# A block-attention and MLP kernel: the newest of a slot's three neighbouring value blocks is loaded by GpSimd, the sampled blocks stay with SyncE

## The chip, the core and the metric

The kernel runs on one core of a Trainium2 chip. The metric is the device time of one execution in microseconds (us), the median of several runs. Engines are named as the profile names them: PE is TensorE, DVE is VectorE, ACT is ScalarE, POOL is GpSimd, SP is SyncE. SP does no arithmetic; it issues transfers. POOL computes and can issue transfers as well.

## The reference, cut to what matters

```python
# attention: 4 batches, 8 heads, 768 rows in 24 blocks of 32, head size 64
scores = scale * q @ k.T
mask = (|blk_i - blk_j| <= 1) | first or last block, of rows or of columns
mask |= blk_j in sampled_blocks[blk_i]        # 3 sampled blocks per block row
attn = softmax(where(mask, scores, -1e9))
out = attn @ v
# then, with x = out as 3072 tokens x 512
h = x @ w_in                                  # 512 x 2048
g = s * maximum(h, 0) ** 2 + b
result = g @ w_out                            # 2048 x 512
```

`sampled_blocks` is an input, so which blocks are sampled is known only when the kernel runs.

## The kernel before, in words

**Slots.** Attention runs in 52 slots, in the order that the table entry "ORD" (L31) gives. Eight dense slots do the two block rows that see every key (the first and the last). The other 44 are sparse: a sparse slot does one of the 22 inner block rows for one of two batch pairs, `e` = 0 or 1 (all eight heads of two batches at once). The block rows of a pair are three streams that walk along neighbouring block rows, A and C upwards, B downwards; while all three are alive their slots alternate C, A, B, and when C has ended only A and B alternate.

**Values of a slot.** A sparse row needs its three neighbouring blocks, the first and last blocks, and three sampled ones. The three neighbours of a stream lie in one row of the tile `vA` (`window_values`), at place j % 3. From one slot of a stream to its next two neighbours stay, and only the newest block comes in, over the one that has gone out: `window_v` (L778), one transfer, 32 partitions x 2 batches x 512 numbers. It may start only when the previous slot of the same stream has finished its product with the values. Only the first slot of a stream in a pair, called `entire` in the code, loads all its window, in several transfers; 21 of the 59 transfers at L778 are of that kind. The sampled blocks go to a ring of five rows, mostly in `vB`, by `sampled_v` (L874, three transfers whose source comes from a register; L871 renews the last block once per ring row in the second pair). Keys are handled alike, but on chip: whole key tiles `kt` are loaded by SP (L697), and POOL copies the newest block (`window_k`, L891) and the sampled ones (`sampled_k`, L902) into the tile `kk`. Queries of the sparse slots are loaded by POOL (L714).

**A sparse slot** then runs so: scores on PE (L958), subtracting the maximum on DVE (L976, results `ptile` and `nm`), exponential on ACT (L989), transposes on PE (L1018; L1016 for dense ones), evacuation by DVE (L1034) or ACT (L1036), the product with `vA` and `vB` on PE into `xs` (`av`, L1075, 64 multiplications), scaling on DVE (L1081), transposes on PE (L1087), a copy on ACT (L1092), and a spill to memory by SP (L1099). Dense slots use L937, L1026 and L1065 in the corresponding places. PE's order per slot i is: transposes of i, last transposes of i - 1, scores of i + 2, product with the values of i.

**Weights.** Beside attention, `decode_f64` (L40) splits blocks of `w_in` and `w_out` into high and low parts: SP loads a raw block in two halves (L59, `raw_i` and `raw_o`), DVE (L85, L87), POOL (L88) and ACT work on it. After attention comes the MLP: products L440 to L442, L482 to L484 and L619 on PE, which read the attention's result back (L400).

**What sets the order.** Each engine runs its instructions in the order in which the program issues them. That order comes from `Plan` (L109), which simulates the engines before anything is issued: each operation has an engine, a cost in ns, a priority (for loads, the slot that needs them less a lead, "VL" 11 for windows and "GV" 13 for sampled blocks) and dependencies. On each engine the earliest possible operation with the smallest priority goes next. The costs steer the order only; on the chip everything waits for its real dependencies, in that order. In the letters of the plan, "s" is SP and "g" is POOL.

Of the kernel before, what the change touches and what calls it, by code (L numbers as in the profile page):

```python
# [108 lines left out]
class Plan:  # L109
# [15 lines left out]
    def op(self, eng, cost, prio, fn, deps=(), alloc=(), use=(), order=(), nbytes=0, cols=0, late=0.0):  # L125


        o = Plan.Op()
        o.cost, o.prio, o.fn, o.nbytes, o.cols, o.late = cost if isinstance(cost, dict) else {eng: cost}, prio, fn, nbytes, cols, late
        o.pick = isinstance(cost, dict)  # L130
        o.deps, o.order, o.alloc = [d for d in deps if d], [d for d in order if d], alloc
        o.end, o.seq = None, len(self.ops)
        for k in (*alloc, *use):
            self.users.setdefault(k, []).append(o)
        self.ops.append(o)
        return o
# [76 lines left out]
def kernel(  # L213
# [16 lines left out]
    nc = tc.nc  # L230
# [432 lines left out]
    with ExitStack() as es:  # L663
# [12 lines left out]
        for w in T["ORD"].split():  # L676
            if w[1] == "D":
                slots.append(("d", "abcd".index(w[0]), int(w[2]), 0))
            else:
                r = "ABC".index(w[1])  # L680
# [37 lines left out]
        def value_tiles():  # L718
            if "A" not in vbox:
                for z in "AB":  # L720
                    vbox[z] = gp.tile([P, 4, 2, DM], F32, tag="vg", name=f"v{z}", bufs=2)

        def window_values(r):
            value_tiles()
            return vbox["A"][:, r]

        def sampled_values(n):
            value_tiles()
            return vbox["B"][:, n - 1] if n else vbox["A"][:, NST]
# [11 lines left out]
        def block_rows(e, j, n=1):  # L741

            return v[2 * e:2 * e + 2, j * BLK:(j + n) * BLK, :].rearrange("a r d -> r a d")

        def newest(k):
            return k - 1 if STREAMS[1] >= k > STREAMS[1] - 8 else k + 1
# [23 lines left out]
        def newcomers(k, entire):  # L770
            return list(range(k - 1, k + 2)) if entire else [newest(k)]

        def window_v(i, entire, m):

            _, e, k, r = slots[i]
            js = newcomers(k, entire)
            j, p = (js[m], js[m] % 3) if m < len(js) else (0, NSL)
            nc.sync.dma_start(out=window_values(r)[p::4], in_=block_rows(e, j))  # L778


        ident = pers.tile([P, P], F32, name="ident")
# [63 lines left out]
        def load_registers(eng):  # L845
            _, regs[eng] = nc.values_load_multi_w_load_instructions(
                packed[0:1, 1:NB - 1], engines=[eng], min_val=0, max_val=NB32 ** NSL - 1, bass_reorder=False,
                skip_runtime_bounds_check_because="three numbers of 0..NB-1, clamped on the chip")

        def block_register(eng, k, a):  # L850

            n = regs[eng][k - 1] >> (5 * a) if a else regs[eng][k - 1]
            return (n & (NB32 - 1) if a < NSL - 1 else n).with_bounds(min_val=0, max_val=NB - 1)
# [4 lines left out]
        def ring_row(what, i):  # L858
            if i not in ring[what]:
                ring[what][i] = len(ring[what]) % {"k": KG, "v": VG}[what]  # L860
            return ring[what][i]

        def sampled_v(i, a):


            _, e, k, r = slots[i]
            row = ring_row("v", i)
            vt = sampled_values(row)
            if a == 0 and holds["v"].get(row) != e:
                holds["v"][row] = e  # L870
                nc.sync.dma_start(out=vt[NSL::4], in_=block_rows(e, NB - 1))  # L871
            src = v[2 * e:2 * e + 2].rearrange("a (n e) d -> n e a d", e=BLK)
            j = block_register(mybir.EngineType.SP, k, a)
            nc.sync.dma_start(out=vt[a::4], in_=src[bass.ds(j, 1)].rearrange("o e a d -> (o e) a d"))  # L874
# [9 lines left out]
        def window_k(i, entire):  # L884

            _, e, k, r = slots[i]
            kk = keys_tile()
            if entire:
                nc.gpsimd.tensor_copy(flat(kk[:, r, NSL:NSL + 1]), flat(kts[e][:, :1]))
            for j, p, n in runs(k, entire):  # L890
                nc.gpsimd.tensor_copy(flat(kk[:, r, p:p + n]), flat(kts[e][:, j:j + n]))  # L891

        def sampled_k(i, a):

            _, e, k, r = slots[i]
            row = ring_row("k", i)
            kg = keys_tile()[:, NST + row]
            if a == 0 and holds["k"].get(row) != e:
                holds["k"][row] = e
                nc.gpsimd.tensor_copy(flat(kg[:, NSL:]), flat(kts[e][:, NB - 1:]))  # L900
            j = block_register(mybir.EngineType.Pool, k, a)
            nc.gpsimd.tensor_copy(flat(kg[:, a:a + 1]), flat(kts[e][:, bass.ds(j, 1)]))  # L902
# [207 lines left out]
        op = plan.op  # L1110
# [27 lines left out]
        o_rs = op("s", 4400, T["RS"], lambda: load_registers(mybir.EngineType.SP), [o_si])  # L1138
# [18 lines left out]
        def parts_of(e, blocks):  # L1157
            return [kld[(e, y, p)] for p in sorted({j * KPS[e] // NB for j in blocks}) for y in range(2)]
# [9 lines left out]
        for i, (kind, e, k, r) in enumerate(slots):  # L1168
            u, cost, col = unit_of[i], costs[kind], cols[kind]
# [21 lines left out]
            if dense:  # L1191
                s_use.append((f"kt{e // 2}", e // 2))
            else:
                prev = before.get(r)
                entire = k == STREAMS[r]
                first = not before
                blocks = [*range(k - 1, k + 2), 0] if entire else [newest(k)]
                new = [("kk", "kk")] if first else []
                pk = op("g", 1900 if entire else 430, u - T["GK"], lambda i=i, w=entire: window_k(i, w),
                        [*parts_of(e, blocks), *(prev[0] if prev else [])], alloc=new, use=[(f"kt{e}", e)] + ([] if first else [("kk", "kk")]), order=[pk])  # L1200
                s_deps.append(pk)
                first_pk = first_pk or pk
                queries()
                for a in range(NSL):
                    pk = op("g", 460, u - T["GK"] + 0.1 * (a + 1), lambda i=i, a=a: sampled_k(i, a), [o_rg, *parts_of(e, range(NB))],
                            alloc=[] if a else [("kg", i)], use=[(f"kt{e}", e), ("kk", "kk")] + ([("kg", i)] if a else []), order=[pk])
                    s_deps.append(pk)
                s_use += [("kk", "kk"), ("kg", i)]

                vt = [("vg", "vA"), ("vg", "vB")]  # L1210
                if first:
                    for m in range(5):
                        pvl = op("s", 450, -8.3 + 0.02 * m, lambda m=m: global_values(m), alloc=[] if m else vt, use=vt if m else [],
                                 order=[pvl], nbytes=(131e3 if m == 4 else 200e3))
                        globs.append(pvl)
                av_deps += globs if e == 0 else []
                for m in range(len(newcomers(k, entire)) + (entire and e > 0)):
                    pvl = op("s", 450, -8.2 + 0.02 * m if first else u - T["VL"] + 0.1 * m, lambda i=i, w=entire, m=m: window_v(i, w, m), prev[1] if prev else [],
                             use=vt, order=[pvl], nbytes=131e3)
                    av_deps.append(pvl)  # L1220
                for a in range(NSL):
                    pvs = op("s", 520, u - T["GV"] + 0.1 * a, lambda i=i, a=a: sampled_v(i, a), [o_rs],
                             alloc=[] if a else [("vs", i)], use=[*vt, *([("vs", i)] if a else [])], order=[pvs], nbytes=131e3)
                    av_deps.append(pvs)
                pv_at.append((u, pvs))
                if 0 <= i - T["K1"] < KPS[1]:
                    key_piece(1, None, i - T["K1"], u - T["GV"] + 0.4, [pvs])
                av_use = [*vt, ("vs", i)]
# [77 lines left out]
            if k % NBC == 1:  # L1306
                left = sum(sl[0] == "s" and sl[1] == e and sl[2] % NBC == 1 for sl in slots[i + 1:])
                done[e] = done.get(e, 0) + 1
                for b in (2 * e, 2 * e + 1):
                    g = (k - 1) // NBC // 6  # L1310
# [95 lines left out]
        for k in range(NPL):  # L1406
            g, f = subs[k]
# [6 lines left out]
            if k > 0:  # L1414
                g, f = subs[k - 1]
# [45 lines left out]
    for i in range(NPL, NSUB):  # L1461
        g, f = subs[i]
# [10 lines left out]
    for s in range(S0, B):  # L1473
        a, b = 2 * s, 2 * s + 1
        for p in range(NFC // 2):
            for n in (1, 2, 6, 7, 5, 3, 4):
                to = product(p, s, n)
                i = None
# [4 lines left out]
                elif n == 2:  # L1483
                    i = take((a, p), to, part_sums["m1"], ALU.add)
# [4 lines left out]
                elif n == 5:  # L1489
                    i = take((b, p + 8), to, part_sums["u2"], ALU.add)  # L1490
                    vec.tensor_tensor(out=part_sums["u3"], in0=to, in1=part_sums["u1"], op=ALU.add)
                elif n == 3:
                    i = take((b, p), to, part_sums["u3"], ALU.add)
                else:
                    i = take((a, p + 8), part_sums["u2"], to, ALU.subtract)
# [93 lines left out]
```

## Time and profile before

| what | value |
|---|---|
| median of three runs | 802.42 us (802.12 to 802.53) |
| profiled execution | 802.29 us |
| its span | 800.5 us |
| mean granted clock of PE | 0.979 |
| busy: PE, DVE, ACT, POOL | 740.6, 573.1, 480.3, 242.1 us |
| transfers on the hardware queue (issued by SP) | 81.76 MB, 34.8% of 16 engines' span |
| transfers on the software queue (issued by POOL) | 6.29 MB, 2.8% |

The span is what the profiler recorded, from the first to the last instruction; the profiled execution's own time is 1.8 us more. Attention takes the first 276 us or so, the MLP the rest. In rows of the timeline the columns are start, length (us), engine, line, operation, output <- inputs, count, and in brackets how long the engine was idle before and what ended that. SPq is the part of SP that issues transfers. In rows of waits there are the engine and its line, what it waited for, and then total us, times, longest us.

### The profile page before, as it was taken

Reading aid. Unit: us, or ns where it says so; the run is one execution under the profiler, and the core shown is the slowest. Engines: PE = TensorE matmul, PEld = TensorE weight load, DVE = VectorE, ACT = ScalarE, POOL = GpSimd, SP = SyncE. Lnnn points to the kernel's source line nnn. Section 1 sums busy time; section 2 is a strip of 40 time slices with the busy share of each in tenths; the row PEclk is TensorE's granted clock in tenths of the full one; section 3 lists DMA queues with packets and bytes.
Section 4 is the critical chain, followed back from the end, with each engine's and each line's share of the span. In section 5 each row is a group of like instructions: output and inputs, shape, how many; then the busy total and the mean of one; then the engine's idle time right before and its main releaser. Section 6 shows DMA issues by size and latency. Waiting matters only on the chain.

```text
span 800.5 us, 21671 instructions
## 1 busy us (share of the span) xinstructions
PE 740.6 (93%) x8096; PEld 632.9 (79%) x8096; DVE 573.1 (72%) x1490; ACT 480.3 (60%) x1181; POOL 242.1 (30%) x398
## 2 busy tenths in 40 slices
PE   7886967779897899999998999999999999999997
PEld 6565756457675799999877998898898998989896
DVE  5865444787777489888799678778667768766762
ACT  3965545678777477788964433476355457534542
POOL 4935225334532021122102322233223223222321
PEclk9999899899999899999999999999999999999999
DMA  8757666754756443553542232035000012000002
GB/s 266 217 165 218 181 192 187 206 158 132 225 169 178 116 144 107 181 178 113 156 118 93 80 123 70 32 80 148 11 0 1 1 40 98 1 1 1 1 0 79
DMA packets 101272, 89.43 MB, mean 112 GB/s; under 512 B 50352, under 2 KB 79664, under 8 KB 101168
## 3 DMA queue, kind: packets, MB, share of 16 engines
q1 hardware_dynamic: 98864, 81.76, 34.8%
q0 software_dynamic: 2304, 6.29, 2.8%
q8 instruction: 64, 1.05, 0.5%
q14 instruction: 40, 0.33, 0.1%
HBM read 69.15 MB, written 14.68 MB: 105 GB/s over the span
## 4 chain that ended last, share of the span: by engine, by line
PE 75%; DVE 8%; ACT 7%; DMA 6%; issue 3%; SPq 1%; ACTq 0%; DVEq 0%
PE m L619 19%; PE o L483 10%; PE o L484 10%; PE o L482 9%; PE t L1018 5%; PE xs L1075 5%; PE s L958 5%; DMA vA<-in_v_dram 4%; PE h L440 2%; ACT ptile L989 2%; PE h L442 2%; PE h L441 2%; PE od L1065 2%; DVE ptile L976 2%; PE xs L1087 1%
## 5 line engine op out<-in xcount | busy, mean ns | idle before, releaser
L461 POOL TENSOR_TENSOR hid<-hid,hid 128x384 fp32r<-128x384 f32 x96 | 106.1, 1106 | 292.4 <-ACT hid L637 251.8
L636 ACT ACTIVATE hid<-hid,sb_b,sb_s 128x384 f32<-128x384 f32 x96 | 68.0, 709 | 151.8 <-DVE hid L630 151.7
L989 ACT ACTIVATE ptile<-ptile,nm 128x256 f32<-128x256 f32 (+2 forms) x224 | 111.4, 501 | 39.0 <-DVE nm L976 38.8
L976 DVE CUSTOM_DVE_ANT_1 ptile<-s,mt 128x256 f32<-128x256 f32 x176 | 64.6, 420 | 27.7 <-PE s L958 26.9
L1075 PE MATMUL xs<-vA,pt 128*32 128x64 f32 x1696 | 49.2, 230 | 30.3 <-DMA vA<-in_v_dram 23.2
L1075 PEld LDWEIGHTS xs<-vA,pt 128*32 128x32 f32 x1696 | 37.5, 115 | 48.6 <-issue 21.4
L484 PE MATMUL o<-woutr,hid 128*128 128x512 f32 x168 | 66.4, 395 | 0.0
L483 PE MATMUL o<-woutr,hid 128*128 128x512 f32 x168 | 66.3, 395 | 0.0
L482 PE MATMUL o<-woutr,hid 128*128 128x512 f32 x168 | 65.3, 389 | 0.0
L619 PE MATMUL m<-wout,win 128*128 128x384 f32 x264 | 62.6, 340 | 2.1 <-ACT xrest L1482 1.6
L619 PE MATMUL m<-xp,wop 128*128 128x384 f32 x288 | 58.3, 337 | 0.0
L1018 PE MATMUL t<-ident,ptile 128*128 128x128 f32 x352 | 57.2, 309 | 0.0
L483 PE MATMUL o<-win,hid 128*128 128x512 f32 x144 | 56.8, 395 | 0.0
L630 DVE SCALAR_TENSOR_TENSOR hid<-hid 128x384 f32<-128x384 f32 x96 | 54.1, 563 | 3.3
L619 PE MATMUL m<-xp,win 128*128 128x384 f32 x288 | 55.1, 338 | 1.4 <-DVE xp L603 0.7
L619 PEld LDWEIGHTS m<-xp,win 128*128 128x128 f32 x288 | 50.9, 188 | 4.6 <-DVE xp L603 1.2
L637 ACT CAST hid<-hid 128x384 fp32r<-128x384 f32 x96 | 49.4, 514 | 7.7 <-ACT hid L636 0.4
L619 PEld LDWEIGHTS m<-xp,wop 128*128 128x128 f32 x288 | 51.5, 188 | 2.1
L1018 PEld LDWEIGHTS t<-ident,ptile 128*128 128x128 f32 x352 | 47.9, 210 | 5.5 <-issue 0.7
L891 POOL COPY kk<-kt 128x256 f32<-128x256 f32 (+2 forms) x46 | 21.4, 469 | 101.9 <-PE s L958 101.9
L619 PEld LDWEIGHTS m<-wout,win 128*128 128x128 f32 x264 | 47.4, 188 | 5.1 <-ACT xrest L1482 2.4
L482 PE MATMUL o<-win,hid 128*128 128x512 f32 x126 | 49.2, 391 | 0.8 <-ACT ob L488 0.7
(192 smaller groups left out, 1885.0 us busy)
## 6 DMA issues: line engine op xcount, KB each, us to landing
vB<-in_v_dram SPq DMA_DIRECT2D x109, 128.0 KB, 3.1
vA<-in_v_dram SPq DMA_DIRECT2D x88, 128.0 KB, 3.3
raw_o<-in_w_out_dram SPq DMA_DIRECT2D x14, 512.0 KB, 3.6
raw_i<-in_w_in_dram SPq DMA_DIRECT2D x12, 512.0 KB, 3.8
xd<-xst SPq DMA_DIRECT2D x44, 128.0 KB, 3.3
out_dram<-ob SPq DMA_DIRECT2D x20, 256.0 KB, 2.1
sum<-xd SPq DMA_DIRECT2D x12, 384.0 KB, 4.5
kt<-in_k_blk_dram SPq DMA_DIRECT2D x8, 384.0 KB, 6.1
```

The costliest lines, as they stand in the source:

```text
L461: (eng or nc.vector).tensor_tensor(out=htile(5 + i % 3), in0=t, in1=gh.bitcast(F32), op=ALU.subtract)
L482: nc.tensor.matmul(acc, gh[:, tsl], wout(f, 0), start=first, stop=False)
L483: nc.tensor.matmul(acc, gh[:, tsl], wout(f, 1), start=False, stop=False)
L484: nc.tensor.matmul(acc, gl[:, tsl], wout(f, 0), start=False, stop=last)
L619: nc.tensor.matmul(to, w_, x_, start=(c == 0 and k == 0), stop=(c == 1 and k == 2))
L630: vec.scalar_tensor_tensor(out=t, in0=t, scalar=0.0, in1=t, op0=ALU.max, op1=ALU.mult)
L636: nc.scalar.activation(t, t, AF.Identity, bias=sb_b, scale=sb_s)
L637: nc.scalar.copy(gh, t)
L976: nc.vector.tensor_tensor_reduce(out=pt, in0=sp, in1=msk, scale=-scale, scalar=FMAX if g == 0 else nm[:, g - 1:g], op0=ALU.add, op1=ALU.mi ...
L989: nc.scalar.activation(pt, pt, AF.Exp, bias=nms[n][:, last:last + 1], scale=-1.0, accum_out=dns[i][:, 2 * g + j:2 * g + j + 1])
L1018: nc.tensor.transpose(tp[:, (2 * j + c) * P:(2 * j + c + 1) * P], src[:, c:SW:2], ident)
L1075: nc.tensor.matmul(xs[quads[pair]], pt[:, c, quads[pair]], vt[:, a, col:col + D], start=(j == 0 and c == 0), stop=(c == 1), tile_position= ...
```

## The change

The transfer of the newest block is issued by POOL instead of SP, for the slots that are not `entire` (38 transfers); the windows of the first slots stay with SP. The planner is told so, with a cost of 650 instead of 450, and the cost of a sampled block's transfer is set from 520 to 800. Nothing else differs.

```diff
@@ window_v
-            nc.sync.dma_start(out=window_values(r)[p::4], in_=block_rows(e, j))
+            (nc.sync if entire else nc.gpsimd).dma_start(out=window_values(r)[p::4], in_=block_rows(e, j))
@@ the plan
                 for m in range(len(newcomers(k, entire)) + (entire and e > 0)):
-                    pvl = op("s", 450, -8.2 + 0.02 * m if first else u - T["VL"] + 0.1 * m, lambda i=i, w=entire, m=m: window_v(i, w, m), prev[1] if prev else [],
+                    pvl = op("s" if entire else "g", 650, -8.2 + 0.02 * m if first else u - T["VL"] + 0.1 * m, lambda i=i, w=entire, m=m: window_v(i, w, m), prev[1] if prev else [],
                              use=vt, order=[pvl], nbytes=131e3)
                     av_deps.append(pvl)
                 for a in range(NSL):
-                    pvs = op("s", 520, u - T["GV"] + 0.1 * a, lambda i=i, a=a: sampled_v(i, a), [o_rs],
+                    pvs = op("s", 800, u - T["GV"] + 0.1 * a, lambda i=i, a=a: sampled_v(i, a), [o_rs],
                              alloc=[] if a else [("vs", i)], use=[*vt, *([("vs", i)] if a else [])], order=[pvs], nbytes=131e3)
```

The orders of PE and ACT stay as they were. Three places on the other engines follow.

SP, late in the sparse slots of the first pair, where the two halves of the first raw weight block (`raw_i`) are loaded among spills (`xd`), sampled blocks (`vB`) and windows (`vA`). Before, then with the change:

```order
L1099 DMA xd_68<-xst20_2478 128x256
L59 DMA raw_i0_2519<-in_w_in_dram 128x2x256
L778 DMA vA_243<-in_v_dram 32x2x512
L871 DMA vB_244<-in_v_dram 32x2x512
L874 REGISTER_ALU
L874 ISA
L874 DMA vB_244<-in_v_dram 32x2x512
```

```order
L1099 DMA xd_68<-xst20_2478 128x256
L59 DMA raw_i0_2531<-in_w_in_dram 128x2x256
L871 DMA vB_244<-in_v_dram 32x2x512
L874 REGISTER_ALU
L874 ISA
L874 DMA vB_244<-in_v_dram 32x2x512
```

The window between the raw load and the sampled blocks is gone from SP; the second raw half still follows three sampled blocks and a spill later, with nothing else put ahead of it.

POOL, at the end of the second pair, around the copies of the newest key (L891) and the sampled keys (L902) for slots 50 and 51 (counted from 0). Before, then with the change:

```order
L891 COPY kk<-kt_830 128x256
L902 REGISTER_ALU
L902 ISA
L902 COPY kk<-kt_830 128x256
L902 REGISTER_ALU x2
L902 ISA
L902 COPY kk<-kt_830 128x256
L902 ISA
L902 COPY kk<-kt_830 128x256
L891 COPY kk<-kt_830 128x256
```

```order
L891 COPY kk<-kt_864 128x256
L902 REGISTER_ALU
L902 ISA
L902 COPY kk<-kt_864 128x256
L902 REGISTER_ALU x2
L902 ISA
L902 COPY kk<-kt_864 128x256
L778 DMA vA<-in_v_dram 32x2x512
L902 ISA
L902 COPY kk<-kt_864 128x256
L891 COPY kk<-kt_864 128x256
```

The window of slot 48 now stands between the second and the third sampled key of slot 50; the third sampled key and the newest key of slot 51 stand behind it. Windows stand among key copies in this way all along POOL's order.

DVE, at the end of the first pair's sparse slots, where the first raw weight block is split (L85, L87) between the maxima of the dense slots (L976). Before, then with the change:

```order
L976 ISA nm91_2726 128x1
L85 TENSOR_SCALAR wkhp0_403<-raw_i0_2519 128x512
L1081 TENSOR_TENSOR xss23_2759<-xs23_2709,rc23_2578 128x256
L87 TENSOR_SCALAR wklp0_588<-raw_i0_2519 128x512
L1081 TENSOR_TENSOR xss0_2778<-od0_879,rc0_414 128x128
L976 ISA ptile0_79,nm92_2787<-s90_2678,mt_128 128x256
```

```order
L976 ISA nm91_2726 128x1
L1081 TENSOR_TENSOR xss23_2755<-xs23_2709,rc23_2575 128x256
L85 TENSOR_SCALAR wkhp0_403<-raw_i0_2531 128x512
L87 TENSOR_SCALAR wklp0_583<-raw_i0_2531 128x512
L1081 TENSOR_TENSOR xss0_2778<-od0_879,rc0_414 128x128
L976 ISA ptile0_79,nm92_2785<-s90_2678,mt_128 128x256
```

One scaling (L1081) now stands ahead of L85 instead of behind it; the next maximum stays behind L85 in both.

## The prediction

> **What bounds the kernel now.** I read the span first, then the chain of waits by engine, then what TensorE (PE) waits for, by stage.
>
> ```profile
> span 800.5 us, 21671 instructions
> PE 75%; DVE 8%; ACT 7%; DMA 6%; issue 3%; SPq 1%; ACTq 0%; DVEq 0%
> PE xs L1075 <- DMA vA<-in_v_dram: 23.2, 9, 5.7
> ```
>
> The profiled execution took 802.29 us: 800.5 of span and 1.8 around it. The median of the runs shown is 802.42, 0.13 more. The chain that ends last is mostly PE work, with 6% of transfers in it. The third row (wait, total, times, longest) names them: nine times the product with the values, `xs` at L1075, stood still for a block of `vA`. Now the same view for three stretches: the sparse slots of the first batch pair (42.4 to 136.8), the second pair (186 to 270), and everything after.
>
> ```profile
> PE xs L1075 <- DMA vA<-in_v_dram: 15.6, 7, 4.5
> PE xs L1075 <- DVE nm L976: 2.7, 2, 1.6
> PE xs L1075 <- ACT ptile L989: 1.3, 1, 1.3
> ...
> PE xs L1075 <- DMA vA<-in_v_dram: 7.5, 2, 5.7
> ...
> PE m L619 <- ACT xrest L1482: 1.6, 2, 1.0
> ```
>
> The first three rows are the first pair's, the fourth the second pair's, the last the largest of six after 276, which come to 4.5 us together. So after attention PE runs almost without a gap: what is won before 276 us arrives at the end, what is lost too.
>
> A wait costs more than its own length. The next view gives stretches: busy time and count for PE, PE's weight loads, DVE, ACT, POOL, then granted clock, DMA share, GB/s.
>
> ```profile
> 80.00:87.00 7.00, 5.23 (x98) 4.36 (x106) 1.37 (x4) 1.46 (x6) 0.00 (x0) 0.51 0.65 204
> 114.00:117.60 3.60, 3.60 (x90) 3.31 (x86) 0.68 (x3) 0.00 (x0) 0.00 (x0) 0.54 0.51 159
> 141.60:148.40 6.80, 4.20 (x30) 2.51 (x31) 5.25 (x20) 2.42 (x10) 1.00 (x1) 0.50 0.60 178
> 216.70:223.40 6.70, 6.02 (x106) 3.90 (x97) 3.57 (x13) 2.65 (x9) 1.52 (x6) 0.50 0.81 248
> 224.00:250.00 26.00, 24.45 (x733) 18.99 (x729) 20.83 (x81) 20.79 (x65) 8.93 (x22) 1.00 0.56 166
> 261.10:267.80 6.70, 5.72 (x105) 5.46 (x106) 1.19 (x3) 0.00 (x0) 0.00 (x0) 0.50 0.44 134
> 42.40:136.80 94.40, 74.78 (x2124) 58.74 (x2122) 50.04 (x214) 51.31 (x178) 33.70 (x84) 0.95 0.65 186
> ```
>
> Undisturbed, PE has the full clock (224 to 250: 1.00). Around a long wait it is granted half for some 6.7 us, so half of the PE time in such a stretch is lost on top. (The Trainium skill, TensorE: Matmul & The Clock Gate, says that an idle array drops to half rate; these rows agree, with a granted clock of 0.50.)
>
> **Why the blocks are late.** SyncE (SP) issues them. Its rows over one slot:
>
> ```profile
> 62.74 0.54 SPq L1099 DMA_DIRECT2D xd<-xst  x1
> 63.32 0.43 SPq L697 DMA_DIRECT2D kt<-in_k_blk_dram  x1
> 63.84 0.63 SPq L778 DMA_DIRECT2D vA<-in_v_dram  x1
> 64.79 2.60 SPq L874 DMA_DIRECT2D vB<-in_v_dram  x3
> 67.48 0.53 SPq L1099 DMA_DIRECT2D xd<-xst  x1
> 68.06 0.43 SPq L697 DMA_DIRECT2D kt<-in_k_blk_dram  x1
> 68.59 0.63 SPq L778 DMA_DIRECT2D vA<-in_v_dram  x1
> ...
> L778 SPq DMA_DIRECT2D vA<-in_v_dram x17: 616/625/1469, 42.4 to 131.2; - x17
> DMA to landing us min/median/max: 2.3/3.4/5.9
> ```
>
> Rows follow each other with no idle time: SP spends 4.7 to 5.3 us a slot in issuing alone (94.4 / 17 is 5.55 with all other loads), while PE's own work is 74.78 / 17 = 4.4. SP is the bound of this stage, and a window, last in its queue, is late because of the queue, not because its place comes free late.
>
> **The change, part by part.** *Removed from SP:* in this stage 17 window issues. 17 x 0.625 = 10.6 us; one took 1.469, 0.85 more; the handover ahead of each (63.32 + 0.43 = 63.75, next row 63.84) is 0.09, so 1.5 in all.
>
> The gain of the first pair isn't what PE waited there, though. Behind the stage stands another SP load:
>
> ```profile
> 131.94 1.49 SPq L871 DMA_DIRECT2D vB<-in_v_dram  x1
> 136.80 0.43 SPq L59 DMA_DIRECT2D raw_i<-in_w_in_dram  x1
> 137.33 0.62 SPq L871 DMA_DIRECT2D vB<-in_v_dram  x1
> 141.99 0.43 DVE L85 TENSOR_SCALAR wkhp<-raw_i 128x512 int32<-128x512 int32 x1 [7.25 <-DMA raw_i<-in_w_in_dram]
> 143.99 0.66 PE L1016 MATMUL t<-ident,ptile 128*128 128x128 f32 x2 [5.07 <-DVE nm L976]
> ```
>
> The second half of weight block `raw_i` is issued at 136.80 and lands in time for DVE at 141.99. DVE stands before it in its fixed order for 7.25 us, so PE has no maximum to go on with for 5.07. This load comes earlier only by what SP is relieved of: 10.6 + 0.85 + 1.5, and 0.9 from the L871 load (1.49 where the next one took 0.62; I count the excess as crowding behind the window issued just before it): 13.9, call it **14.0**. PE, free of its `vA` waits, arrives some 24 us earlier (15.6 + 2.7 + 1.3 of waits, and half of 5.23 and of 3.60 at half clock: 2.6 + 1.8). The difference of 10 reappears as a longer wait at this place: about 15 us for PE instead of 5.07. Whatever sampled loads become late on SP before it is inside the same sum, since the raw load ends the stage. The longer idle lets more of the half-clock stretch fill with work: (6.8 - 4.2) / 2 = 1.3 lost.
>
> *Second pair.* Here two windows alone are late, and only they:
>
> ```profile
> 215.47 0.62 PE L1075 MATMUL xs<-vA,pt 128*32 128x64 f32 x8 [1.80 <-DMA vA<-in_v_dram]
> ...
> 249.74 0.31 PE L1075 MATMUL xs<-vB,pt 128*32 128x64 f32 x8
> ...
> 254.06 2.72 SPq L874 DMA_DIRECT2D vB<-in_v_dram  x3
> 258.56 0.62 SPq L778 DMA_DIRECT2D vA<-in_v_dram  x1
> 262.08 1.94 PE L1075 MATMUL xs<-vA,pt 128*32 128x64 f32 x64 [5.75 <-DMA vA<-in_v_dram]
> ```
>
> The window of 258.56 could have gone once the previous product of its stream had ended, at about 250.05 (249.74 + 0.31). It stood 8.5 us behind other SP issues. From POOL it is issued near 250.7 and lands near 255, before PE wants it at 256.3 (262.08 - 5.75). The wait of 1.80 goes likewise. With the half-clock stretches: 1.80 + 6.02 / 2 + 5.75 + 5.72 / 2 = **13.4**.
>
> *Added to POOL:* 38 issues. The nearest rows are POOL's own query loads and its key copies:
>
> ```profile
> L714 POOL DMA_DIRECT2D qr_4s<-in_q_dup_dram x8: 615/616/868, 17.0 to 110.7; - x8
> DMA to landing us min/median/max: 2.6/4.3/5.8
> ...
> 62.39 0.40 POOL L891 COPY kk<-kt 128x256 f32<-128x256 f32 x1 [3.25 <-PE s L958]
> 62.73 1.09 POOL L902 COPY kk<-kt 128x256 f32 x3
> ```
>
> I take 0.62 per issue: POOL then has 0.40 + 1.09 + 0.62 = 2.1 us a slot, beside the 3.25 that it waits for scores. Ends for the issue: 0.62 and, unseen here, a stretch as below. Landing takes 4.3 rather than 3.4; in three-stream stages a window has two whole slots, over 8 us, between its place coming free and its use, so this is hidden; at the two-stream end 6.3 us are there for 4.9. *Added wait:* the window on POOL waits for the stream's previous product; behind it stand a sampled-key copy and the next slot's newest key. These serve scores that PE reaches two or three slots later, and POOL's keys already wait for an earlier score, so I price it at 0. If that cover fails it costs a late key per slot, some 0.6 us, the length of the issue. *Moved rows:* PE's and ACT's orders stay; on DVE L85 falls one 0.42 us row later, hidden by its own wait for `raw_i`. The two planner costs have no other effect.
>
> Sum: 802.29 - 14.0 - 13.4 + 1.3 = **776.2**.
>
> A rule that speaks against it: the Trainium skill, DMA: Bandwidth & Descriptors, section Issuing engines are not separate DMA queues, says that all issuers share 16 DMA engines and that issuing from several saves only the sequencer's time, usually small. By that rule the gain is SP's time alone; here that time is measured at 0.62 a piece and is what the stage lacks, with the DMA share at 0.65, so row and rule give the same 14.0 in the first pair.
>
> **The rivals.**
> *PE alone bounds.* SP's fast issues let the raw load keep up with PE: gains 24 + 13.4 = 37.4, **764.9**. For: part of SP's time may be waits in disguise. Against: SP's rows have no gaps.
> *Other loads take over.* Sampled blocks, which stay on SP, or windows landing late from POOL, hold PE in the second pair too. Then 10.6 in the first pair and some 4 of the 13.4 remain, with the 1.3 lost: 802.29 - 13.3 = **789.0**. For: 4 us is all that a 1.80 wait with part of its stretch is worth, and in the second pair raw loads and spills crowd SP. Against: only `vA` appears in the waits.
> *No effect.* The transfers themselves are late, whoever issues them: landing rises from 3.4 to 4.3 and by more in crowded moments (up to 5.8), and the 9 late windows stay late: **802**, within 0.2%. Against: a queue of 8.5 us against a landing of 3.4.
> *Slower: POOL's issues stretch.* POOL must write what the DMA engines read. If DVE's work holds it up, an issue takes long, and the keys behind it come late. POOL's slot is 1.49 us of copies plus the issue; above 3.8 us per issue it exceeds SP's 5.3, and decides. At 4.5 it costs (6.0 - 5.3) x 17 = 12 us: **814**. Against: 616 ns median and 868 at most over the L714 group, with DVE busy for half the time (50.04 of 94.40). (The Trainium skill, SBUF — State Buffer, tells of such a case: about 620 ns alone, about 3100 ns beside a DVE copy. By 3.1, the slot would be 4.6 and still not decide; no row here shows it.)
>
> **How the numbers follow.** Forecast 55%, its own range 770 to 783 (the bounds of the raw term, 10.6 to 16). PE alone 15%, other loads 20%, no effect 4%, slower 6%. The range must reach from PE alone to other loads: 765 to 790. About 0.2% is what a measurement of this kernel can tell from no change; faster by more than that 0.90, within it 0.04, slower 0.06.
>
> **What would show it.** On SP between 42 and 131, no L778 row and slots of about 4.6 us. PE's wait for `vA` gone from both stretches; PE at L1016 waiting about 15 us for DVE's maximum, DVE at L85 about as long or longer for `raw_i`. L778 on POOL at 0.62 each; POOL's key copies still released by scores. In the second pair no half-clock stretch at 216 and 261. The forecast is wrong if the wait before L1016 stays at 5, if `vB` appears among PE's waits beyond a few us, or if POOL's issues take over 1 us.

## The result, and the profile after

The changed kernel takes 778.05 us (median of four runs, 773.99 to 780.49), the kernel before, in the same comparison, 802.27: a ratio of 0.97, 95% interval 0.9647 to 0.9752. That is 24.2 us less; 26.1 were forecast. The profiled execution took 780.49 us with a span of 778.7, so it stands 21.8 under the 802.29 of before, and the steps below are measured against that 21.8.

First the span and the chain of waits by engine, then PE's waits in the first pair's sparse slots with the dense slot behind them (36 to 142 us), and in the second pair (176 to 262).

```profile
span 778.7 us, 21689 instructions
PE 79%; DVE 8%; ACT 6%; issue 3%; DMA 2%; SPq 1%; ACTq 0%; DVEq 0%
```

```profile
PE t L1016 <- DVE nm L976: 9.3, 1, 9.3
PE s L958 <- issue: 2.6, 1, 2.6
...
PE xs L1087 <- DVE xss L1081: 3.5, 4, 1.4
PE xs L1075 <- issue: 2.4, 3, 1.0
```

PE's waits for `vA`, 23.2 us before, are gone from the list. In their place stand one wait of 9.3 for DVE's maximum, one of 2.6 at the scores, and small ones in the second pair. The next rows show the windows on POOL: count, then minimum, median and maximum in ns, then the time from issue to landing.

```profile
L778 POOL DMA_DIRECT2D vA<-in_v_dram x38: 537/546/565, 38.6 to 250.5; - x38
...
DMA to landing us min/median/max: 2.3/3.4/5.6
```

And the timeline at the place where the forecast put the new bound: PE's last work before the wait and its first after, SP's second raw half, DVE at L85.

```profile
120.09 1.53 PE L1016 MATMUL t<-ident,ptile 128*128 128x128 f32 x12
130.91 0.66 PE L1016 MATMUL t<-ident,ptile 128*128 128x128 f32 x2 [9.29 <-DVE nm L976]
...
125.39 0.42 SPq L59 DMA_DIRECT2D raw_i<-in_w_in_dram  x1
...
128.90 0.43 DVE L85 TENSOR_SCALAR wkhp<-raw_i 128x512 int32<-128x512 int32 x1 [9.33 <-DMA raw_i<-in_w_in_dram]
```

PE comes to this place 17.3 us earlier than before (120.09 against 137.40), the raw load is issued 11.4 earlier (125.39 against 136.80), and PE goes on 13.1 earlier (130.91 against 143.99). So 4 of PE's 17 us are given back here. The load itself was also quicker: from its issue to DVE's start went 3.5 us (125.39 to 128.90), where it had been 5.2 (136.80 to 141.99). Two markers bound the rest: the scores of one slot early in the second pair, and those of its last slot. Before:

```profile
212.58 1.09 PE L958 MATMUL s<-kk,qr_3s 64*32 64x256 f32 x32
...
268.05 1.09 PE L958 MATMUL s<-kk,qr_2s 64*32 64x256 f32 x32
```

and with the change:

```profile
199.65 1.09 PE L958 MATMUL s<-kk,qr_3s 64*32 64x256 f32 x32
...
247.00 1.09 PE L958 MATMUL s<-kk,qr_2s 64*32 64x256 f32 x32
```

The first is 12.9 us earlier, the last 21.05: the second pair gave 8.1. The remaining 0.75 of the 21.8 came behind the last marker.

### The profile page after: what moved, and what is told of

The parts are those of the page before. It is cut to its first block, busy times and chain, and to the rows that moved or that the text cites. A ratio compares the mean times of both kernels' runs of the same rounds, so it can differ in the third digit from the quotient of the medians.

```text
span 778.7 us, 21689 instructions
## 1 busy us (share of the span) xinstructions
PE 736.9 (95%) x8096; PEld 628.9 (81%) x8096; DVE 575.6 (74%) x1490; ACT 479.8 (62%) x1181; POOL 263.7 (34%) x436
## 4 chain that ended last, share of the span: by engine, by line
PE 79%; DVE 8%; ACT 6%; issue 3%; DMA 2%; SPq 1%; ACTq 0%; DVEq 0%
PE m L619 19%; PE o L483 10%; PE o L484 10%; PE o L482 10%; PE t L1018 6%; PE s L958 6%; PE xs L1075 6%; PE h L440 2%; PE h L442 2%; PE h L441 2%; PE od L1065 2%; ACT ptile L989 2%; PE xs L1087 1%; PE t L1016 1%; DVE ptile L976 1%
## 5 line engine op out<-in xcount | busy, mean ns | idle before, releaser
L976 DVE CUSTOM_DVE_ANT_1 ptile<-s,mt 128x256 f32<-128x256 f32 x176 | 64.7, 420 | 28.2 <-PE s L958 27.4
L1075 PEld LDWEIGHTS xs<-vA,pt 128*32 128x32 f32 x1696 | 35.3, 111 | 22.7 <-ACT xst L1092 9.0
L1075 PE MATMUL xs<-vA,pt 128*32 128x64 f32 x1696 | 47.7, 224 | 3.4 <-issue 1.8
L902 POOL COPY kk<-kt 128x256 f32 x132 | 49.9, 408 | 0.1
```

Source lines behind the costliest of these rows:

```text
L976: nc.vector.tensor_tensor_reduce(out=pt, in0=sp, in1=msk, scale=-scale, scalar=FMAX if g == 0 else nm[:, g - 1:g], op0=ALU.add, op1=ALU.mi ...
L1075: nc.tensor.matmul(xs[quads[pair]], pt[:, c, quads[pair]], vt[:, a, col:col + D], start=(j == 0 and c == 0), stop=(c == 1), tile_position= ...
```

## The experiments

The kernels ran in three groups, each with the kernel before beside it; its median was 801.91, 799.76 and 798.54 us, so groups are compared by the ratio to it.

| kernel | us, median (range of 4; 10 for the fifth) | ratio, 95% interval |
|---|---|---|
| first pair's windows on POOL | 785.32 (784.87 to 787.9) | 0.9799 (0.9766 to 0.9833) |
| second pair's windows on POOL | 793.09 (786.68 to 796.09) | 0.9872 (0.9818 to 0.9925) |
| the change, SP issues an extra transfer instead | 792.22 (790.48 to 794.92) | 0.988 (0.9845 to 0.9916) |
| the change, L85 later | 773.76 (772.15 to 775.45) | 0.965 (0.9616 to 0.9685) |
| before, L85 later | 796.99 (793.33 to 801.96) | 0.996 (0.9935 to 0.9985) |
| the change, old planner costs | 776.08 (774.77 to 776.65) | 0.9693 (0.9663 to 0.9723) |
| L85 later, all second-pair windows on POOL | 771.67 (770.73 to 777.11) | 0.9666 (0.9621 to 0.9711) |
| L85 later, spills on ACT | 780.11 (778.25 to 782.5) | 0.9755 (0.9718 to 0.9792) |
| the change again | 775.37 (773.76 to 778.48) | 0.9692 (0.9659 to 0.9725) |
| both raw blocks later, spills on ACT | 773.66 (771.58 to 774.54) | 0.9681 (0.9652 to 0.9709) |
| the same, all second-pair windows on POOL | 770.29 (768.78 to 772.24) | 0.9641 (0.9608 to 0.9674) |
| both raw blocks later, all second-pair windows on POOL, spills on SP | 770.26 (766.41 to 776.21) | 0.9659 (0.9606 to 0.9713) |

### One pair at a time

```diff
-            (nc.sync if entire else nc.gpsimd).dma_start(...)
+            (nc.sync if entire or e != 0 else nc.gpsimd).dma_start(...)   # and the planner's engine likewise
```

> Only the first batch pair's windows go to POOL; the second pair's stay on SP, with the planner's costs of the changed kernel. Theory (two separate gains: SP relieved ahead of the raw load in the first pair, two late windows in the second): about 13 us faster than before, 789 us (787 to 792), with the waits of PE for vA in the second pair still there, 5 to 8 us. Rival (the first pair's gain alone carries it all, or the second's alone): 778, or 802.

785.32. PE's waits in the trace: the one ahead of L1016, and in the second pair still a late window.

```profile
129.08 0.66 PE L1016 MATMUL t<-ident,ptile 128*128 128x128 f32 x2 [8.94 <-DVE nm L976]
...
248.14 1.93 PE L1075 MATMUL xs<-vA,pt 128*32 128x64 f32 x64 [7.45 <-DMA vA<-in_v_dram]
```

The mirror image has `e != 1`, and the planner's costs of before:

> Only the second pair's windows go to POOL, with the planner's costs of before, so the first pair's order stays that of before. Theory: the first pair keeps its 15 us of waits for vA and its wait of 5 us ahead of L1016; the second loses its two waits: 802.3 less 9 to 13, so 789 to 793 us. Rival (the second pair's windows were late only because of what the first pair left behind on SP): 800 to 803.

793.09, with 16.8 us of waits for `vA` in the first pair, where the kernel before has 15.6, and none in the second:

```profile
PE xs L1075 <- DMA vA<-in_v_dram: 16.8, 7, 5.3
PE t L1016 <- DVE nm L976: 8.7, 9, 4.5
```

The two alone give 801.91 - 785.32 = 16.6 and 8.8 us, together 25.4, the size of the whole change. So there are two separate gains, and neither makes the other. The first came out 2 us beyond its expected 787 to 792.

### Windows on POOL, SP as loaded as before

```diff
         def window_v(i, entire, m):
...
+        extra = lambda i: nc.sync.dma_start(out=dd[i], in_=block_rows(slots[i][1], newest(slots[i][2])))
...
-                    av_deps.append(pvl)
+                    av_deps.append(pvl); entire or op("s", 450, u - T["VL"], lambda i=i: extra(i), prev[1] if prev else [])
...
-                    pvs = op("s", 800,
+                    pvs = op("s", 520,
```

> As the change, but SP issues another transfer of a value block of the same size, to memory that nobody reads, where the window stood, and the sampled cost is 520 again, so SP's order is that of before almost row for row. Theory (in the first pair the raw load behind SP's queue sets the end): PE no longer waits for vA, yet the raw load comes no earlier than before, about 135 to 137; PE's wait ahead of L1016 grows to about 20 us and the first pair gains 0 to 3; with the second pair's 9 to 13 that gives 787 to 793 us. Rival (what counts is that the windows are there in time, SP's relief is worth nothing): 778, as the change.

792.22. SP's second raw half, DVE, and PE, then the two markers of the second pair:

```profile
134.99 0.42 SPq L59 DMA_DIRECT2D raw_i<-in_w_in_dram  x1
...
138.23 0.43 DVE L85 TENSOR_SCALAR wkhp<-raw_i 128x512 int32<-128x512 int32 x1 [10.69 <-DMA vB<-in_v_dram]
...
140.24 0.66 PE L1016 MATMUL t<-ident,ptile 128*128 128x128 f32 x2 [10.65 <-DVE nm L976]
...
209.81 1.09 PE L958 MATMUL s<-kk,qr_3s 64*32 64x256 f32 x32
...
255.16 1.09 PE L958 MATMUL s<-kk,qr_2s 64*32 64x256 f32 x32
```

No wait for `vA` is left, and still the first pair gains next to nothing: the early marker is 2.8 us ahead of before (212.58 to 209.81), against 12.9 with the change. The raw half is issued at 134.99; taking the 17 extra issues away brings it to 125.39, or to 124.10 in the second profile of the change further down: 9.6 or 10.9 us, 0.56 or 0.64 each. That is what SP's issuing costs the first pair, apart from the windows being in time. (The releaser that the profile names at L85 is a `vB` load; the input of L85 is the raw block, whose second half landed 3.1 us after its issue, and DVE went on at 3.2.) The second pair gains 12.9 - 2.8 = 10.1, whatever SP carries: there the window's place in the queue counted.

Two numbers missed. PE's wait ahead of L1016 was 10.65, not 20, because PE came late itself: ACT's copy at L1092 stood four times for a spill in SP's queue, and PE behind it (all of it between 36 and 142 us).

```profile
PE xs L1075 <- ACT xst L1092: 5.2, 2, 2.7
...
ACT xst L1092 <- DMA xd<-xst: 9.2, 4, 3.6
```

And the span is 793.2, only 7.3 under before, where the last marker is 12.9 early: between attention and MLP, where spills stood between extra transfers, the same copy held PE again and the half clock followed. Together 5.6 us were given back; the rows show 1.97 of wait and some 2.2 at the lower clock (0.45 of 4.80), and the rest isn't placed.

```profile
267.19 0.47 PE L1087 MATMUL od<-ident,xss 128*128 128x128 f32 x1 [1.97 <-ACT xst L1092]
...
266.00:272.00 6.00, 4.80 (x74) 4.32 (x75) 1.43 (x3) 1.41 (x4) 0.00 (x0) 0.55 0.77 178
```

### DVE's instruction out of the way

```diff
-    nbytes=524e3 / pieces, late=T["LATE"])
+    nbytes=524e3 / pieces, late=T["LATE"] + 16e3 * (k == 0))
```

`late` is time that the planner adds to a raw load's landing; SP's order stays, L85 moves some 60 rows down DVE's, and the later steps of that block move with it, on ACT too.

> The changed kernel with the first raw block counted 16 us later by the planner, so that L85 stands some 60 rows later in DVE's order; SP's loads stay where they are. Theory (in-order DVE stands at L85 for a raw load that PE doesn't need yet): PE's 9.3 us ahead of L1016 go, and the half clock behind it, 5.88 / 2 = 2.9: about 12 us faster than the change, 766 us (764 to 770). Rival (SP's sampled blocks are as late as the raw load): the wait moves to vB at L1075, 775 to 778 us.

773.76, a ratio of 0.965 where the change has 0.97 and 0.9692: about 4 us, not 12, and the intervals overlap, so the times alone leave its size open. In the trace the wait ahead of L1016 is gone, and a new one stands a few us behind it. PE's row, ACT's row that held it, and SP's queue ahead of the spill that ACT waited for:

```profile
138.78 0.90 PE L937 MATMUL s<-kt,qr_0d 64*64 64x192 f32 x4 [5.18 <-ACT wkhp L1028]
...
138.08 0.27 ACT L1092 COPY xst<-od 128x128 f32<-128x128 f32 x1 [5.52 <-DMA xd<-xst]
...
129.53 2.30 SPq L874 DMA_DIRECT2D vB<-in_v_dram  x2
131.93 2.67 SPq L778 DMA_DIRECT2D vA<-in_v_dram  x4
134.84 0.62 SPq L874 DMA_DIRECT2D vB<-in_v_dram  x1
135.56 0.53 SPq L1099 DMA_DIRECT2D xd<-xst  x1
```

The copy at L1092 needs one of four `xst` buffers; the spill that frees it is issued at 135.56, behind sampled blocks and the second pair's first windows. So the rival had the right idea (another load behind SP's queue takes over) in the wrong place. The same edit on the kernel before:

> The kernel before, windows on SP, with the first raw block counted 16 us later by the planner, so that L85 stands later on DVE. Theory: PE's 5.07 us ahead of L1016 go, with up to 2.1 of half clock; but as in the run with the change, the copy at L1092 waits next, for a spill behind SP's queue, so 1 to 5 us faster than before, 797 to 801, and the waits for vA stay at 15 to 17 us. Rival (the raw load is no bound of its own in the kernel before): no change, 802.

796.99 against 799.76: 2.8 us, with an interval that leaves out no change, as expected. PE's waits for `vA` were still 14.7 us in all, and 4.6 came at L937 for the same reason as above.

### The planner's costs

The change with 450 and 520 in place of 650 and 800.

> The change without its two planner costs: windows on POOL, counted 450 and 520 as before. Theory (the costs only order rows; the engine counts): 776 to 781 us, as the change. Rival (the planner's order makes a good part of the gain): 785 us or more.

776.08, a ratio of 0.9693. The costs make no difference that these runs can tell.

### After L85: windows and spills

All second-pair windows on POOL, the first ones too:

```diff
-            (nc.sync if entire else nc.gpsimd).dma_start(...)
+            (nc.sync if entire and e == 0 else nc.gpsimd).dma_start(...)   # and the planner's engine likewise
```

> The changed kernel with L85 later, and also the whole first windows of the second pair on POOL. Theory (with L85 out of the way, PE stands 5.18 us at L937 behind the copy of L1092, which waits for a spill issued at 135.56 behind four windows, 2.67 us, on SP): the spill comes about 2.7 us earlier and with it PE: 770 to 772 us against 773.8. Rival (the sampled blocks ahead of the spill hold it, not the windows): 773 to 775.

771.67, but by ratio 0.9666 against 0.965: the times don't show a gain. The trace shows what was meant to happen: ACT's wait shrinks from 5.52 to 3.86, with the copy at 135.01 instead of 138.08.

```profile
135.01 0.27 ACT L1092 COPY xst<-od 128x128 f32<-128x128 f32 x1 [3.86 <-DMA xd<-xst]
```

Spills of sparse slots issued by ACT, in another run:

```diff
-                nc.sync.dma_start(out=xd[b, hf, :, m]..., in_=xst)
+                nc.scalar.dma_start(out=xd[b, hf, :, m]..., in_=xst)   # and the planner's engine likewise
```

> The changed kernel with L85 later, and the sparse slots' spills issued by ACT instead of SP. Theory (SP's queue is still what PE waits for, by way of spills): the copies at L1092 no longer wait for a buffer, the 5.18 us at L937 go, and SP is relieved of 0.53 a slot: 764 to 769 us. Rival (ACT, in order, spends 0.5 us a slot on issuing ahead of exponentials that PE needs): 774 us or slower.

780.11, slower than with L85 later alone. The longest wait of PE was for the next raw block, which had taken the place of the first.

```profile
153.42 0.43 DVE L85 TENSOR_SCALAR wkhp<-raw_o 128x512 int32<-128x512 int32 x1 [11.17 <-DMA raw_o<-in_w_out_dram]
...
155.32 1.87 PE L937 MATMUL s<-kt,qr_0d 64*64 64x288 f32 x12 [10.38 <-DVE dp L1026]
```

The last group delays the second raw block also (`16e3 * (k < 2)`).

> L85 later and spills on ACT, as in the run that took 780.11, with the second raw block (raw_o) also counted 16 us later by the planner. Theory (in that run DVE stood 11.17 us at L85 for raw_o, and PE 10.4 behind it; moving spills to ACT was not what cost the time): the 10.4 us go with some half clock, 767 to 771 us. Rival (ACT's issues cost the time): 777 us or more.

773.66, ratio 0.9681 against 0.9755: the 10.4 us wait is gone and with it some 6 us, with intervals that don't meet. So most of the loss was that wait; the time lies between the theory's 767 to 771 and the rival's 777. But it is no better than L85 later with the spills on SP (0.965), so the times show no gain from moving the spills, and PE now stands 4.9 us for `vA` and `vB` in the first pair (3.1 and 1.8), for sampled blocks that SP loads, where L85 later alone has no such wait.

> The same with the second pair's first windows on POOL too. Theory (what SP issues between the pairs is still waited for): 2 us faster than without, 765 to 769. Rival (SP is no longer waited for): equal to the run without.

770.29 against 773.66 in the same group: 3.4 us where the theory had 2, though the time is above its 765 to 769, and the intervals overlap a little.

> L85 later and all second-pair windows on POOL, as in the run that took 771.67, with raw_o also later. Theory (there DVE does not stand at L85 for raw_o, since SP's queue is short): no change, 770 to 773. Rival: 767 or less.

770.26: no change by time, as expected, though its four runs spread over 10 us. The last two are about 5 us under the change of the same group (775.37), with overlapping intervals; by ratio L85 later alone (0.965) is as fast.

### The change again

> The changed kernel once more, unedited, for a second profile, since its four times lie 6.5 us apart (774.0 to 780.5). Theory (the time of the raw load's landing, and so PE's wait ahead of L1016, differs from run to run): again 774 to 781 us, with PE's wait there between 7 and 11 us. Rival (the first profile shows an outlier): below 775 with hardly a wait there.

775.37, 773.76 to 778.48. The wait is there again, shorter:

```profile
130.89 0.66 PE L1016 MATMUL t<-ident,ptile 128*128 128x128 f32 x2 [7.66 <-DVE nm L976]
...
124.10 0.42 SPq L59 DMA_DIRECT2D raw_i<-in_w_in_dram  x1
...
128.88 0.43 DVE L85 TENSOR_SCALAR wkhp<-raw_i 128x512 int32<-128x512 int32 x1 [7.71 <-DMA vB<-in_v_dram]
...
199.17 1.09 PE L958 MATMUL s<-kk,qr_3s 64*32 64x256 f32 x32
...
244.97 1.09 PE L958 MATMUL s<-kk,qr_2s 64*32 64x256 f32 x32
```

Here the raw half is issued 12.7 us earlier than before, 1.3 more than in the first profile; yet DVE and PE go on at the same time as there (128.88 and 130.89, against 128.90 and 130.91), since from issue to DVE's start went 4.8 us instead of 3.5. So the theory put the spread of the runs at the wrong place. Of the 2.0 us between the two spans (778.7 and 776.7) the early marker has 0.5 and the last one all; what differs in the second pair stays open. That pair gives 23.1 - 13.4 = 9.7 here.

## Why the prediction was right, step by step

Of the 26.1 us that were forecast the profile has 21.8: 12.9 where 12.7 were put, 8.1 where 13.4 were, and 0.75 behind the last marker.

**The bound in the first pair: right, and the size partly by luck.** The step said that the raw load behind SP's queue, not PE's waits for `vA`, sets the gain, 14.0 less 1.3 for the half clock: 12.7. PE went on 13.1 earlier, and 12.9 had arrived at the early marker. But the load was issued only 11.4 and 12.7 earlier in the two profiles. The rest of the 13.1 came from its time to DVE's start, 3.5 and 4.8 us where it had been 5.2, which the sum didn't have, and hardly any of the 1.3 shows. The run with the extra issue says why less than 14: the 17 issues are worth 9.6 to 10.9, about the 10.6 counted for them, and little is left for the 0.85, 1.5 and 0.9 that were added. With windows on POOL and SP as full as before the first pair gains 2.8, and that too goes with the raw load: it was issued 1.8 earlier and DVE went on 3.8 earlier (138.23).

**The wait that takes the place: right in place, too long by a third or more.** Forecast about 15 us ahead of L1016; measured 9.3 and 7.7. The reason is PE's arrival, put 24 us earlier and in fact 17.3. Some 5.6 of the missing 6.7 are at one place, where PE's scores stopped and the clock fell:

```profile
81.86 1.07 PE L958 MATMUL s<-kk,qr_1s 64*32 64x256 f32 x7 [2.55 <-issue]
...
79.00:82.00 3.00, 0.45 (x13) 0.14 (x6) 0.43 (x2) 0.97 (x3) 0.90 (x3) 0.94 0.99 313
82.00:85.00 3.00, 3.00 (x76) 2.02 (x74) 1.26 (x7) 1.48 (x6) 1.09 (x3) 0.50 0.67 199
85.00:88.00 3.00, 3.00 (x39) 2.88 (x38) 0.74 (x4) 0.10 (x2) 0.97 (x2) 0.50 0.62 193
```

That is 2.55 of wait and half of 6.0 at half clock. The profile names no releaser ("issue"). The queries of these scores were there: the last of their four loads, which POOL issues behind a window at 69.47, landed 5.9 us later. The transfers were busy 0.99 of the time, and among them are 16 KB ones on a queue that the profile calls instruction (q8). One of these ended at 80.35, 1.5 us before PE went on. All five stops of PE of more than 0.4 us without a releaser in this profile (36 to 262) ended 1.4 to 1.5 us after such a transfer, and in four other runs PE stopped at this same multiplication, for 0.70 to 2.28 us, again until 1.4 to 1.5 us after one. So PE probably stood for its own next instructions, late among full transfers; no run here changes that to prove it. It cost nothing at the end, since the raw load came later still.

**The second pair: right in kind, too large.** Forecast 13.4; measured 8.1 and 9.7, 10.1 with the extra issue. Both waits for `vA` went, 1.80 and 5.75, and the half clock behind them. The step that failed is that nothing takes their place: PE's small waits of this stage grew, at L1087 and L1075 together 5.9 where they had been 3.2 (2.3, 0.5 and 0.4); of the 5.9, 2.4 are stops without a releaser, as above. And a stretch at 0.72 of the clock appeared, worth some 1.3, so that about 4 of the missing 5.3 are found in the first profile:

```profile
226.00:232.00 6.00, 4.56 (x89) 2.73 (x83) 3.33 (x11) 3.22 (x10) 2.13 (x5) 0.72 0.60 164
```

**POOL's price: right.** 0.62 was taken for an issue, 0.546 was measured, with DVE (the third pair of numbers) busy 51.97 of 79.3 us in the first pair's slots. The windows waited for PE's products on POOL, 32.6 us in all, and PE's list has no wait for a copied key:

```profile
42.40:121.70 79.30, 75.74 (x2135) 58.81 (x2133) 51.97 (x214) 51.58 (x179) 44.47 (x102) 0.96 0.71 214
...
POOL vA L778 <- PE od L1065: 22.2, 13, 4.3
POOL vA L778 <- PE xs L1075: 10.4, 9, 3.6
POOL kk L891 <- PE s L958: 50.1, 29, 3.6
```

POOL's wait for scores fell from 101.9 to 50.1: windows used idle time. Landing took 3.4, not 4.3.

**The rivals.** PE alone as the bound (764.9): PE did arrive 17 us early, and was stopped; the runs with L85 later show that removing one SP-fed wait brings up the next. Other loads taking over (789.0): with the change, PE's list has no wait for `vA` or `vB`, and the second pair kept 8 to 10 us, not 4. No effect: the waits went, with the landing at 3.4 us as before. Stretched issues on POOL: longest 565 ns, nowhere near the 3.8 us at which they would decide. The Trainium skill (DMA: Bandwidth & Descriptors, section Issuing engines are not separate DMA queues) says that issuing from several engines saves only the sequencer's time, usually small relative to the transfer itself. The first pair agrees: an issue took about 0.6 us against 3.4 to landing, and 17 of them made 9.6 to 10.9 us, because that sequencer was what the stage lacked.

## What to carry to other kernels

When a queue is full, the gain of moving work off it is read not from the waits it causes most often but from the last thing in that queue that somebody stands for, here a weight load that an in-order DVE waited for: PE came 17 us earlier there, and 13 were kept. Keep the two effects apart with a run that leaves the old queue as full as it was: here, with SP as full as before, 3 us came in the first pair and 10 in the second, and the queue's relief was worth another 10 in the first. And an instruction that isn't needed yet, but stands in an in-order engine ahead of one that is, is worth moving down: here it gave 3 and 6 us in two comparisons, and about 4 in a third whose intervals overlap.

## What the runs showed of the hardware that was not expected

A window of 128 KB took 546 ns to issue on POOL and 608 on SP with the change (616 before). A spill of 128 KB took 326 ns on ACT and, in the kernel before, 533 on SP:

```profile
L778 SPq DMA_DIRECT2D vA<-in_v_dram x21: 599/608/732, 15.9 to 152.1; - x21
...
L1099 ACTq DMA_DIRECT2D xd<-xst x44: 326/326/391, 39.6 to 258.0; - x44
L1099 SPq DMA_DIRECT2D xd<-xst x44: 326/533/3436, 46.5 to 281.5; - x44
```

The quickest spill on SP took 326 ns as well, so it isn't the engine alone that makes the difference; what does wasn't tried. And the stops of PE without a releaser, above, follow the transfers on the instruction queue.
